# An attention and Fourier-mixing kernel: a shallower pair pipeline, row means from the residual add, held loads, and Fourier pieces emitted together

## The chip, the cores and the metric

One core of a Trainium2 chip runs the whole problem. The time is device microseconds (us) of one execution; the kernel before has a median of 345.32 us over 3 runs (344.11 to 345.38). Engines are named as the profile names them: PE is TensorE (PEld its weight loads), DVE VectorE, ACT ScalarE, POOL GpSimd, SP SyncE, which here only issues DMAs.

## What is computed

Block-sparse attention for 4 batches of 8 heads (768 positions, head size 64), then a Fourier mixing layer and a two-layer network over the 512 features that the heads form together. Inputs and output are float32.

```python
k_rep = k.reshape(B, H, 12, 64, D).mean(axis=3)
gate_scores = q . k_rep, with later blocks set to -1e9
sel = the 3 best blocks of each row, and its own block
attn = softmax(q k^T / 8, over the selected blocks and causal)   # then attn @ v
x = attn output as (batch, 768, 512)
u = x + real(fft over features of (fft over positions of x))
un = (u - mean(u)) / sqrt(var(u) + 1e-6)        # over the 512 features
out = u + relu(un @ w_ch1) @ w_ch2
```

## The kernel before

Heads are taken two at a time: 16 pairs P, four to a batch b. A pair goes through these stages, each a Python function that emits instructions.

- `stage_A(P)` transposes k and then q by PE (12 transposes, L239). For k, DVE sums the blocks (L242, `kr`) and ACT copies the tile to float16 (L245 for pairs under 7, L248 after); for q, DVE copies (L253) and POOL converts (L170).
- `stage_G(P)` is the gate: PE scores each row against the blocks (L300 or L266), and DVE turns them into a mask: a transpose, ten or twelve MAX8, two small products and a transpose (L307 to L315, or L272 to L281).
- `stage_S(P, 0)` to `stage_S(P, 5)` are the six score tiles: PE (L339, L344, masks L350), exponential on ACT (L354), causal edge on POOL (L357).
- `stage_V(P, 0)` and `(P, 1)` multiply with v on PE (L370); after the second, DVE takes the reciprocal (L379) and writes x (L167 `x`). `stage_fold` prepares the Fourier input on DVE (`sd` for each pair, `zw` for the third and fourth pair of a batch).

When all four pairs of a batch are folded its stream follows: `stage_fg` (DVE), `stage_Y(b, 0)` and `(b, 1)` (PE L423 and L429, out by ACT L436 `ty` and DVE L438 `tr`), `stage_M(b, 0)` to `(b, 2)`, `stage_R` (the reciprocal square root, DVE and POOL), 16 `stage_W1` tiles (L503, L505; ReLU on ACT L512 or DVE L510) and 6 `stage_W2` tiles (L521; DVE adds the residual at L527, SP stores at L530). `stage_M(b, kp)` covers 256 rows: 8 matmuls, one DVE add `u = mixed + x` of 1024 columns (L458), two `bn_stats` and `bn_aggr` (L468, L469), the scaled mean (L471), two ACT passes that write the centred rows (L474), and two DMA transposes on SP into `unT` (L477). W1 needs `unT`. In L167 `u` is that add, because all such adds share one helper line.

All PSUM tiles come from one pool of four buffers (`pst`), each two banks: a fifth tile waits for one of the four before it to be read.

What sets the order. `attn_slot(i, g, a)` lists the pieces of one slot: scores of pair i, gate of pair g, `stage_A` of pair a with its loads for pair a + 3 behind it, and `stage_V` of pair i - 1. Before, g is i + 2 and a is i + 3 up to slot 3, slot 4 has no `stage_A`, slot 5 has no gate, and from slot 6 on they are i + 1 and i + 2. Slots 0 to 4 run alone. From slot 5 on `weave` mixes the slots of four pairs with one batch's stream, by the weights that stand beside each piece; `stream` also puts the last four W2 tiles of the batch before (`held`) behind `stage_fg` and `stage_R`. The opening (L669 to L682) runs in exactly the order written on all engines; after it only SP does, and on the other engines Tile's scheduler takes the pieces by their place in the list and by what its plan says is ready. SP issues every load of q, k and v (`load`, L216 and L209) and every `unT` transpose, so a load emitted ahead of a transpose is issued ahead of it. W1 and W2 weights are loaded by POOL in four chunks each, gated on a pair's scores (`load_w1`, `load_w2`).

Of the kernel before, what the change touches and what calls it, by code (L numbers as in the profile page):

```python
# [20 lines left out]
DM = 512  # L21
# [107 lines left out]
def kernel(  # L129
# [99 lines left out]
    def stage_A(P):  # L229
# [5 lines left out]
        for who in (1, 0):  # L235
# [4 lines left out]
            if who == 1:  # L240
# [3 lines left out]
                if P < NX:  # L244
                    nc.scalar.copy(out=qk[:, 1, XW(P), :], in_=ps)  # L245
                else:
                    for e in range(2):
                        nc.scalar.copy(out=qk[0:64, e, 1, :], in_=ps[64 * e:64 * e + 64])  # L248
# [194 lines left out]
    def stage_M(b, kp):  # L443
# [3 lines left out]
        for k2 in range(2):  # L447
# [9 lines left out]
        kk = slice(2 * kp, 2 * kp + 2)  # L457
        tt(u_b.rearrange("p k (m two) -> p k two m", two=2),  # L458
           mps.rearrange("p k (two m) -> p k two m", two=2),
           x_b[:, kk, :].rearrange("p k (m two) -> p k two m", two=2), ALU.add)  # L460
        if kp == 0:
            un_t[b] = bpool.tile([128, NDT, S], F16, tag="unT", name=f"unT_{b}", bufs=1)
            st_t[b] = [bpool.tile([128, *sh], FP, tag=n, name=f"{n}_{b}", bufs=2)
                       for n, sh in (("mv", [NST, 2]), ("rs", [NST]))]
        mv = st_t[b][0]
        for k2 in range(2):
            bst = spool.tile([128, 6], FP, tag="bst", name=f"bst{2 * kp + k2}_{b}", bufs=4)
            nc.vector.bn_stats(out=bst, in_=u_b[:, k2, :])  # L468
            nc.vector.bn_aggr(out=mv[:, 2 * kp + k2, :], in_=bst)  # L469
        nm = spool.tile([128, 2], FP, tag="nm", name=f"nm{kp}_{b}")  # L470
        nc.vector.tensor_scalar(out=nm, in0=mv[:, kk, 0], scalar1=-0.0625, scalar2=None,  # L471
                                op0=ALU.mult)
# [103 lines left out]

    def load_w1(dt, P):
# [12 lines left out]
    def attn_slot(i, g, a):  # L590
# [78 lines left out]
    with tc.manual_schedule(engines={ET.SP, ET.PE, ET.DVE, ET.Activation, ET.Pool}):  # L669
# [62 lines left out]
```

## Time and profile before

| What | Value |
|---|---|
| median of 3 runs | 345.32 us (344.11 to 345.38) |
| the profiled execution's own time | 343.65 us |
| its span, first to last instruction | 341.9 us |
| busy: PE, DVE, ACT, POOL | 304.9, 190.4, 164.7, 114.7 us |
| mean granted TensorE clock | 0.955 of full |

A profile row gives a time from the start of the span, a duration, and in square brackets how long the engine was idle before it and what ended that. PE's ends are modelled, so PE can be shown busy for somewhat longer than a matmul holds it. In the rows by stretch each engine has its busy time and, in brackets, its instructions; PEclk is the granted clock as a share of 2.4 GHz, so 0.50 is 1.2 GHz throughout.

### The profile page before, as it was taken

How to read it: one execution, taken by the hardware profiler on the slowest of the kernel's cores; microseconds unless marked ns; L12 is line 12 of the kernel's file. 1: busy time of each engine (PE TensorE's matmuls, PEld its weight loads, DVE VectorE, ACT ScalarE, POOL GpSimd, SP SyncE). 2: the span in 40 equal slices, each digit the busy share in tenths (PEclk: the TensorE clock that was granted, in tenths of full speed). 3: DMA queues.
4: the chain of work that ended last, by engine and by line, in shares of the span. 5: the costliest groups of instructions: out<-in, count | busy, mean ns of one | idle time of the engine just before them, and what ended most of it. 6: DMA issues, size and time to landing. Idle time of an engine off the chain costs nothing.

```text
span 341.9 us, 6605 instructions
## 1 busy us (share of the span) xinstructions
PE 304.9 (89%) x2594; PEld 180.1 (53%) x2594; DVE 190.4 (56%) x534; ACT 164.7 (48%) x203; POOL 114.7 (34%) x257
## 2 busy tenths in 40 slices
PE   7579787776999999969999999989999999599994
PEld 3356554454556555725666555645665463266441
DVE  2678886597457367892546376974414478021211
ACT  2327776448486643473757634375664024145000
POOL 2436467535544443336362423245110001100000
PEclk9859998896999999989999999999999999899999
DMA  9999999993772544039930004045000102600022
GB/s 175 219 229 265 229 213 211 217 179 65 138 140 46 105 92 110 3 61 229 188 63 0 2 0 110 2 94 169 0 2 0 63 0 58 159 0 2 0 82 104
DMA packets 95371, 34.40 MB, mean 101 GB/s; under 512 B 89120, under 2 KB 91500, under 8 KB 95340
## 3 DMA queue, kind: packets, MB, share of 16 engines
q1 hardware_dynamic: 90460, 29.26, 40.2%
q0 software_dynamic: 2688, 4.19, 6.9%
q10 hardware_dynamic: 2192, 0.52, 0.8%
q8 instruction: 20, 0.33, 0.4%
q14 instruction: 11, 0.09, 0.1%
HBM read 28.73 MB, written 6.29 MB: 102 GB/s over the span
## 4 chain that ended last, share of the span: by engine, by line
PE 67%; DVE 21%; ACT 7%; issue 2%; DMA 2%; SPq 0%; POOL 0%; DVEq 0%
PE c L521 18%; PE h L503 16%; PE h L505 8%; PE av L370 5%; PE sc L344 5%; DVE bst L468 4%; DVE u L167 3%; PE tp L239 2%; PE yp L423 2%; DVE kr L242 2%; DVE x L167 2%; DMA unT<-x 2%; PE g L300 2%; PE sc L339 2%; ACT pt L354 2%
## 5 line engine op out<-in xcount | busy, mean ns | idle before, releaser
L354 ACT ACTIVATE pt<-sc 128x1024 f16<-128x1024 f32 x96 | 84.8, 920 | 46.7 <-PE sc L344 37.8
L521 PE MATMUL c<-w_sb,hT 128*128 128x512 f16 x384 | 88.2, 382 | 1.7 <-ACT pt L354 1.1
L503 PE MATMUL h<-unT,w_sb 128*128 128x512 f16 x256 | 87.1, 385 | 1.8 <-DMA unT<-x 1.8
L505 PE MATMUL h<-unT,w_sb 128*128 128x256 f16 x256 | 69.9, 276 | 2.5 <-DMA unT<-x 2.5
L357 POOL TENSOR_SCALAR_AFFINE_SELECT pt<-pt 128x256 f16<-128x256 f16 x96 | 40.2, 426 | 92.6 <-ACT pt L354 91.8
L521 PEld LDWEIGHTS <-hT 128*128 128x128 f16 x384 | 37.3, 98 | 44.5 <-issue 4.2
L512 ACT ACTIVATE hT<-h 128x768 f16<-128x768 f32 x48 | 38.7, 812 | 36.2 <-PE h L505 35.8
L510 DVE TENSOR_SCALAR hT<-h 128x768 f16<-128x768 f32 x16 | 15.3, 956 | 48.2 <-PE h L505 48.2
L503 PEld LDWEIGHTS <-w_sb 128*128 128x128 f16 x256 | 25.2, 99 | 30.4 <-issue 4.6
L527 DVE SCALAR_TENSOR_TENSOR u<-c,rs,u 128x512 f32<-128x512 f32 x24 | 17.1, 742 | 35.5 <-PE c L521 35.5
L170 POOL TENSOR_SCALAR_AFFINE_SELECT qk<-q 64x768 f16<-64x768 f32 (+1 forms) x25 | 21.6, 866 | 28.0 <-DVE q L253 24.7
L344 PE MATMUL sc<-qk 96*128 96x512 f16 (+3 forms) x144 | 27.8, 306 | 2.7 <-DVE q L253 1.3
L505 PEld LDWEIGHTS <-w_sb 128*128 128x128 f16 x256 | 25.3, 99 | 8.4 <-DMA unT<-x 3.5
L370 PEld LDWEIGHTS <-pt 128*128 128x128 f16 x672 | 25.9, 100 | 5.7 <-issue 1.5
L239 PE MATMUL tp<-id,nat 128*128 128x128 f32 x192 | 26.4, 285 | 2.6 <-issue 1.6
L370 PE MATMUL av<-v,pt 128*128 128x65 f16 x672 | 28.0, 198 | 0.3 <-POOL pt L357 0.3
L474 ACT ACTIVATE x<-u,nm 128x512 f16<-128x512 f32 x24 | 15.8, 713 | 20.7 <-DVE nm L471 20.7
L239 PEld LDWEIGHTS tp<-id,nat 128*128 128x128 f32 x192 | 22.0, 146 | 6.5 <-issue 3.7
L339 PE MATMUL sc<-qk 64*128 64x512 f16 (+3 forms) x112 | 16.7, 338 | 7.6 <-ACT qk L245 3.9
L170 POOL TENSOR_SCALAR_AFFINE_SELECT qk<-mt 32x384 f16<-32x384 f16 x36 | 18.3, 508 | 7.5 <-DVE mt L281 5.8
L344 PEld LDWEIGHTS <-qk 96*128 96x128 f16 x144 | 12.9, 97 | 12.1 <-issue 3.3
L248 ACT CAST qk<-tp 64x768 f16<-64x768 f32 x18 | 14.3, 792 | 8.7 <-DVE kr L242 8.6
(81 smaller groups left out, 335.6 us busy)
## 6 DMA issues: line engine op xcount, KB each, us to landing
nat<-in_k_dram SPq DMA_DIRECT2D x32, 192.0 KB, 4.4
nat<-in_v_dram SPq DMA_DIRECT2D x16, 384.0 KB, 6.4
nat<-in_q_dram SPq DMA_DIRECT2D x30, 192.0 KB, 4.3
out_dram<-u SPq DMA_DIRECT2D x11, 512.0 KB, 3.3
w_sb<-in_moe_w_ch_dram POOLq DMA_DIRECT2D x8, 512.0 KB, 7.4
fs_sb<-c_FS SPq DMA_DIRECT2D x1, 582.0 KB, 4.8
out_dram<-u SPq DMA_DIRECT2D x2, 256.0 KB
nat<-in_q_dram ACTq DMA_DIRECT2D x2, 192.0 KB, 5.4
```

What stands on the lines that cost most here:

```text
L170: nc.gpsimd.affine_select(out=out, in_=in_, pattern=[[0, i] for i in n], base=0, channel_multiplier=0, compare_op=ALU.is_ge, fill=0.0)
L239: nc.tensor.transpose(ps[:, 128 * st:128 * st + 128], src[:, st, :], id32)
L339: nc.tensor.matmul(ps[:, e, co:co + q1 - q0], qk[hs[e], 1, XW(P), 128 * jt:128 * jt + 128], qk[hs[e], 0, XW(P), q0:q1], start=(co == 0), s ...
L344: nc.tensor.matmul(ps[:, e, co:co + q1 - q0], qk[0:96, e, 1, 128 * jt:128 * jt + 128], qk[0:96, e, 0, q0:q1], start=True, stop=True)
L354: nc.scalar.activation(out=pt[:, o:o + 2 * n].rearrange("p (e c) -> p e c", e=2), in_=ps[:, :, 0:n], func=AF.Exp, scale=0.125)
L357: nc.gpsimd.affine_select(out=dg, in_=dg, pattern=[[0, 2], [1, 128]], base=0, channel_multiplier=-1, compare_op=ALU.is_ge, fill=0.0)
L370: nc.tensor.matmul(av[:, e, 66 * st:66 * st + 65], pt[:, co:co + 128], vv[:, e, jt, 0:65], start=(cnt == 0), stop=(cnt == 20))
L503: nc.tensor.matmul(hp[:, 0:512], w1s, unT[:, dt, 0:512], start=(dt == 0), stop=(dt == NDT - 1))
L505: nc.tensor.matmul(hp[:, 512:768], w1s, unT[:, dt, 512:768], start=(dt == 0), stop=(dt == NDT - 1))
L512: nc.scalar.activation(out=hT, in_=hp, func=AF.Relu)
L521: nc.tensor.matmul(cps[:, part, :], h_t[b, it][:, 128 * st:128 * (st + 1)], w2_sb[:, it, :], start=(it == 0), stop=(it == NIT - 1))
L527: nc.vector.scalar_tensor_tensor(out=o[:, i, :], in0=cps[:, i, :], scalar=st_t[b][1][:, sts[i]:sts[i] + 1], in1=o[:, i, :], op0=ALU.mult, ...
```

## The change

Four things are altered.

1. The order of the pairs. The opening emits all six score tiles of pair 0 between `stage_G(1)` and the end of `stage_A(2)`, and the ACT copy of k of pair 1 is emitted after the first two of them (`later`). Slot 0 is gone. Slots 1 to 4, and all after, take gate i + 1 and `stage_A` i + 2. Inside a slot `stage_A` moves up to behind `stage_S(i, 1)`, and each half of `stage_V` moves back by one score tile.
2. `stage_M` has, for each half of 512 columns, one scalar_tensor_tensor whose accumulator gives the row sum, where one 1024-wide add, two bn_stats and two bn_aggr stood; the scaled mean comes from that sum. The bn_stats and bn_aggr move to `stage_R`.
3. `hold_loads` and `free_loads`: SP's loads that fall between them go on a list and are issued behind the batch's last `unT` transpose. In batch 0 holding starts at slot 4.
4. Weights in `stream`: `stage_Y` 0.5 for 1.3, `stage_M` 0.3 for 0.87, `stage_R` 10 (batch 0) or 3 for 6 or 1, so that the Y and M pieces come closer together in the list and W1 comes later. W2's chunks are gated on pairs 5 and 6, not 4 and 5.

```diff
     def load(P, who, eng):
+        if hold[0] is not None:
+            hold[0].append((P, who, eng))
+            return
...
                 if P < NX:
-                    nc.scalar.copy(out=qk[:, 1, XW(P), :], in_=ps)
+                    cp = (lambda ps=ps: nc.scalar.copy(out=qk[:, 1, XW(P), :], in_=ps))
+                    if later is None:
+                        cp()
+                    else:
+                        later.append(cp)
...
-        tt(u_b.rearrange("p k (m two) -> p k two m", two=2),
-           mps.rearrange("p k (two m) -> p k two m", two=2),
-           x_b[:, kk, :].rearrange("p k (m two) -> p k two m", two=2), ALU.add)
...
         for k2 in range(2):
-            bst = spool.tile([128, 6], FP, tag="bst", name=f"bst{2 * kp + k2}_{b}", bufs=4)
-            nc.vector.bn_stats(out=bst, in_=u_b[:, k2, :])
-            nc.vector.bn_aggr(out=mv[:, 2 * kp + k2, :], in_=bst)
+            kt = 2 * kp + k2
+            nc.vector.scalar_tensor_tensor(
+                out=u_b[:, k2, :].rearrange("p (m two) -> p two m", two=2),
+                in0=mps[:, k2, :].rearrange("p (two m) -> p two m", two=2), scalar=1.0,
+                in1=x_b[:, kt, :].rearrange("p (m two) -> p two m", two=2),
+                op0=ALU.mult, op1=ALU.add, accum_out=sm[:, kt:kt + 1])
         nm = spool.tile([128, 2], FP, tag="nm", name=f"nm{kp}_{b}")
-        nc.vector.tensor_scalar(out=nm, in0=mv[:, kk, 0], scalar1=-0.0625, scalar2=None,
-                                op0=ALU.mult)
+        nc.vector.tensor_scalar(out=nm, in0=sm[:, 2 * kp:2 * kp + 2],
+                                scalar1=-0.0625 / DM, scalar2=None, op0=ALU.mult)
...
     def stage_R(b):
-        mv, rs = st_t[b]
+        mv, rs, _ = st_t[b]
+        for kt in range(NST):
+            bst = spool.tile([128, 6], FP, tag="bst", name=f"bst{kt}_{b}", bufs=4)
+            nc.vector.bn_stats(out=bst, in_=u_t[b, kt // 2][:, kt % 2, :])
+            nc.vector.bn_aggr(out=mv[:, kt, :], in_=bst)
...
+    def hold_loads():
+        hold[0] = hold[0] or []
+
+    def free_loads():
+        L, hold[0] = hold[0], None
+        for x in L or []:
+            load(*x)
...
         add(i - 1, 0.0, lambda: cast_v(i - 1))
-        if i > 0:
-            add(i, 0.45, lambda: stage_S(i, 0))
+        add(i, 0.45, lambda: stage_S(i, 0))
         add(g, 0.4, lambda: stage_G(g))
-        if i > 0:
-            add(i, 0.45, lambda: stage_S(i, 1))
+        add(i, 0.45, lambda: stage_S(i, 1))
+        add(a, 1.3, sa)
+        add(i, 0.45, lambda: stage_S(i, 2))
         add(i - 1, 0.6, lambda: stage_V(i - 1, 0))
         if g is not None and g >= NX:
             add(g, 0.0, lambda: stage_K(g))
-        add(i, 0.45, lambda: stage_S(i, 2))
+        add(i, 0.45, lambda: stage_S(i, 3))
         add(i - 1, 0.6, v1)
-        add(i, 0.45, lambda: stage_S(i, 3))
-        add(a, 1.3, sa)
         add(i, 0.45, lambda: stage_S(i, 4))
         add(i, 0.12, lambda: stage_S(i, 5))
...
-        L = [(lambda: stage_fg(b), 0.0)] + held[0:1]
-        L += [(lambda h=h: stage_Y(b, h), 1.3) for h in range(2)]
-        L += [(lambda kp=kp: stage_M(b, kp), 0.87) for kp in range(3)]
-        L += [(lambda: stage_R(b), 6.0 if b == 0 else 1.0)]
+        L = [(hold_loads, 0.0), (lambda: stage_fg(b), 0.0)] + held[0:1]
+        L += [(lambda h=h: stage_Y(b, h), 0.5) for h in range(2)]
+        L += [(lambda kp=kp: stage_M(b, kp), 0.3) for kp in range(3)]
+        L += [(free_loads, 0.0), (lambda: stage_R(b), 10.0 if b == 0 else 3.0)]
         L += held[1:]
         if b == 0:
-            L += [(lambda c=c: load_w2(c, 4 + c // 2), 0.0) for c in range(4)]
+            L += [(lambda c=c: load_w2(c, 5 + c // 2), 0.0) for c in range(4)]
...
-        stage_A(1)
+        later = []
+        stage_A(1, later)
         stage_S(0, 0)
         stage_S(0, 1)
+        later[0]()
         stage_G(1)
         kq(4)
         load(1, 2, nc.sync)
+        stage_S(0, 2)
+        stage_S(0, 3)
         stage_A(2)
+        stage_S(0, 4)
+        stage_S(0, 5)
...
-        run(attn_slot(0, 2, 3))
         load_w1(0, 0)
-        run(attn_slot(1, 3, 4))
+        run(attn_slot(1, 2, 3))
...
-        run(attn_slot(4, 6, None))
+        hold_loads()
+        run(attn_slot(4, 5, 6))
...
-                L += attn_slot(i, *((None, 7) if i == 5 else (i + 1, i + 2)))
+                L += attn_slot(i, i + 1, i + 2)
```

## Rows read from the trace of the kernel before

**Rows 1.** The page: the span and each engine's busy time.

```profile
span 341.9 us, 6605 instructions
PE 304.9 (89%) x2594; PEld 180.1 (53%) x2594; DVE 190.4 (56%) x534; ACT 164.7 (48%) x203; POOL 114.7 (34%) x257
```

**Rows 2.** By stretch: start:end, length, PE, PEld, DVE, ACT, POOL, clock, DMA, GB/s.

```profile
28.00:35.60 7.60, 6.50 (x110) 4.38 (x104) 6.00 (x21) 5.93 (x8) 4.96 (x11) 1.00 1.14 281
43.20:51.90 8.70, 6.64 (x108) 4.47 (x104) 7.34 (x23) 6.93 (x10) 5.81 (x13) 1.00 1.08 215
73.00:79.00 6.00, 2.10 (x23) 1.43 (x23) 6.00 (x13) 4.58 (x7) 2.51 (x4) 1.00 0.53 104
79.00:86.20 7.20, 5.83 (x68) 3.45 (x65) 4.72 (x24) 4.79 (x7) 5.11 (x17) 0.54 0.39 61
146.00:150.00 4.00, 2.06 (x11) 0.78 (x8) 4.00 (x11) 3.30 (x6) 1.29 (x2) 1.00 0.17 33
150.00:154.00 4.00, 2.90 (x19) 0.92 (x18) 3.55 (x17) 3.45 (x5) 1.53 (x4) 0.66 0.49 100
170.00:205.00 35.00, 34.97 (x300) 21.46 (x299) 19.13 (x56) 20.56 (x26) 14.43 (x26) 1.00 0.13 22
220.00:225.00 5.00, 3.93 (x26) 2.42 (x25) 5.00 (x15) 3.51 (x6) 0.41 (x1) 1.00 0.26 52
292.00:298.00 6.00, 3.52 (x14) 1.54 (x12) 0.00 (x0) 0.43 (x1) 0.22 (x2) 0.72 0.76 203
```

**Rows 3.** Timeline, PE and DVE, opening and slot 1: start, us, instruction, [idle before].

```profile
17.00 2.82 PE L239 MATMUL tp<-id,nat 128*128 128x128 f32 x12
29.05 0.52 DVE L307 STREAM_TRANSPOSE gt<-g 128x320 f32<-128x320 f32 x1 [1.32 <-PE g L304]
30.72 0.81 PE L370 MATMUL av<-v,pt 128*128 128x65 f16 x21
32.83 0.63 DVE L167 TENSOR_TENSOR sd<-x 128x384 f16<-128x384 f16 x2
35.21 0.39 PE L339 MATMUL sc<-qk 64*128 64x512 f16 x2 [1.10 <-ACT qk L245]
36.59 0.52 DVE L307 STREAM_TRANSPOSE gt<-g 128x320 f32<-128x320 f32 x1 [1.31 <-PE g L304]
```

**Rows 4.** The chain that ended last, 56 to 90 us: start, us, what.

```profile
60.65 0.64 DVE fg L167
66.84 1.04 ACT ty L436
78.49 0.85 DVE kr L242
82.89 3.25 DMA unT<-x
```

**Rows 5.** Groups by line: count | busy us, mean ns of one | idle before.

```profile
L468 DVE BATCH_NORM_STATS2 bst<-u 128x6 f32<-128x512 f32 x24 | 15.4, 677 | 0.0
L469 DVE BATCH_NORM_AGGREGATE mv<-bst 128x2 f32<-128x6 f32 x24 | 3.7, 166 | 0.0
L167 DVE TENSOR_TENSOR u<-mx,x 128x1024 f32<-128x1024 f32 x12 | 14.3, 1205 | 0.0
L527 DVE SCALAR_TENSOR_TENSOR u<-c,rs,u 128x512 f32<-128x512 f32 x24 | 17.1, 742 | 35.5 <-PE c L521 35.5
```

**Rows 6.** One line, the transposes into unT: count, duration ns min/median/max.

```profile
L477 SPq DMA_TRANSPOSE unT<-x x24: 1189/1217/2141, 73.6 to 291.6; - x24
```

**Rows 7.** The chain from 275 to 300 us, then PE's timeline there.

```profile
279.35 2.32 DVE u L167 x2
291.58 3.53 DMA unT<-x
...
295.15 0.40 PE L505 MATMUL h<-unT,w_sb 128*128 128x256 f16 x1 [2.48 <-DMA unT<-x]
```

**Rows 8.** Timeline of POOL at 49 us: v's cast and its load.

```profile
49.09 0.90 POOL L170 TENSOR_SCALAR_AFFINE_SELECT v<-nat 128x768 f16<-128x768 f32 x1 [0.17 <-DMA nat<-in_v_dram]
```

More of the change, by code (lines that the diff above doesn't have):

```diff
@@ L202 @@
     x_t, u_t, un_t, h_t, st_t = {}, {}, {}, {}, {}
+    hold = [None]
     def load(P, who, eng):
+        if hold[0] is not None:
+            hold[0].append((P, who, eng))
+            return
         b, hp = divmod(P, NP)
@@ L227, in XW, with stage_A @@
         return 1 if P in (0, 1, 2, 6) else 0
-    def stage_A(P):
+    def stage_A(P, later=None):
         d = pairs[P]
@@ L456, in stage_M @@
                                  stop=True)
-        kk = slice(2 * kp, 2 * kp + 2)
-        tt(u_b.rearrange("p k (m two) -> p k two m", two=2),
-           mps.rearrange("p k (two m) -> p k two m", two=2),
-           x_b[:, kk, :].rearrange("p k (m two) -> p k two m", two=2), ALU.add)
         if kp == 0:
@@ L463, in stage_M @@
             st_t[b] = [bpool.tile([128, *sh], FP, tag=n, name=f"{n}_{b}", bufs=2)
-                       for n, sh in (("mv", [NST, 2]), ("rs", [NST]))]
-        mv = st_t[b][0]
+                       for n, sh in (("mv", [NST, 2]), ("rs", [NST]), ("sm", [NST]))]
+        sm = st_t[b][2]
         for k2 in range(2):
-            bst = spool.tile([128, 6], FP, tag="bst", name=f"bst{2 * kp + k2}_{b}", bufs=4)
-            nc.vector.bn_stats(out=bst, in_=u_b[:, k2, :])
-            nc.vector.bn_aggr(out=mv[:, 2 * kp + k2, :], in_=bst)
+            kt = 2 * kp + k2
[4 more added lines that the diff above has]
+                op0=ALU.mult, op1=ALU.add, accum_out=sm[:, kt:kt + 1])
         nm = spool.tile([128, 2], FP, tag="nm", name=f"nm{kp}_{b}")
-        nc.vector.tensor_scalar(out=nm, in0=mv[:, kk, 0], scalar1=-0.0625, scalar2=None,
-                                op0=ALU.mult)
+        nc.vector.tensor_scalar(out=nm, in0=sm[:, 2 * kp:2 * kp + 2],
+                                scalar1=-0.0625 / DM, scalar2=None, op0=ALU.mult)
         for k2 in range(2):
@@ L686 @@
         nc.sync.dma_start(fd_sb, dr["FD"].ap())
-        run(attn_slot(0, 2, 3))
         load_w1(0, 0)
-        run(attn_slot(1, 3, 4))
+        run(attn_slot(1, 2, 3))
         load_w1(1, 1)
-        run(attn_slot(2, 4, 5))
+        run(attn_slot(2, 3, 4))
         load_w1(2, 2)
-        run(attn_slot(3, 5, 6))
+        run(attn_slot(3, 4, 5))
         load_w1(3, 3)
         consts_next()
-        run(attn_slot(4, 6, None))
+        hold_loads()
+        run(attn_slot(4, 5, 6))
         for b in range(B):
```

## The prediction, made before the change was run

> **What bounds the kernel now.** I read the page first: PE is busy 304.9 us of a span of 341.9 [rows 1], so the first question is where the other 37 us lie, and where PE runs at half clock. Busy time by stretch answers that. From 170 to 205 us PE is full at the granted clock of 1.00 [rows 2]; of such stretches (86 to 130 and 298 to 325 look the same) nothing can be won by moving work. The idle time sits in five other places, each with a limit of its own.
>
> First the attention-only stretch, up to the first Fourier piece at 60.65 us [rows 4]. A slot there takes 7.54 us, from one gate transpose at 29.05 to the next at 36.59 [rows 3], with PE busy 6.50, DVE 6.00, ACT 5.93 of 7.6 [rows 2]: no engine is full. DVE waits 1.3 us for the gate's matmuls once a slot and PE waits 1.10 us for the ACT copy of k to free a PSUM buffer [rows 3]. It is a loop of dependences: gate, mask, x, fold, k sums, copy of k, next scores. Slot 3, where the fold has a second step, takes 8.7 us [rows 2].
>
> Then the Fourier chain of each batch, read in the chain that ended last and in the same stretches. For batch 0 it runs from 60.65 to the last transpose landing at 82.89 + 3.25 = 86.1 us, 25.5 us, and other work stands in it: the k sums of the next pair at 78.49, ahead of the last rows' mean [rows 4]. DVE is full from 73 to 79 while PE is idle 3.9 us, and the next 7.2 us have 1.4 idle at a clock of 0.54 [rows 2]. Batch 1 shows the same from 146 to 154 (3.0 idle, the second half at 0.66), batch 2 has 1.1 from 220 to 225 [rows 2]. In batch 3 nothing is left beside the chain but W2: W1's second matmul group waits 2.48 us for `unT` at 295.15 [rows 7], and the stretch after 292 runs at 0.72 [rows 2].
>
> **The change, part by part.**
>
> (a) Shallower pairs. The opening now holds the scores of pair 0, so one whole slot goes; its gate 2 and pair 3 move to slot 1, where old slot 1 had gate 3 and pair 4, and gate 6 moves behind the Y pieces. In the opening pair 2's 12 transposes ran from 17.00 to 19.8 [rows 3]. They now stand behind two score tiles, estimated at 0.8 each (twice the 0.39 us of such a tile [rows 3], the most that the lower clock level can make of it), and behind a gate that may be up to 1.0 later, as the copy of k follows two exponentials. So they end near 22.4, and with the copy of q slot 1 starts near 23.6. A new slot lies between PE's 6.50 [rows 2] and, if a new loop closes, 8.1 (rival 1). `stage_A` in front of V lets the next gate's matmuls run while DVE does x and the fold, so the old 1.3 us wait should shrink to about 0.9, while PE no longer queues behind the k copy at the slot's start: I take 7.2, and 8.1 for the two slots with the second fold step. Then the Fourier pieces start at 23.6 + 7.2 + 7.2 + 8.1 + 8.1 = 54.2, 6.4 ahead of 60.65; less gate 6 on PE, which comes later (some 0.8 of the 1.4 us from 35.21 to 36.59 [rows 3]), **5.6**. With 6.5 a slot (plus 0.9 twice) it is 10, with 8.1 (plus 0.9 twice) it is 2.8; less 0.8 each, 2 to 9.
>
> (b) Means from the add. Before, a half of u cost DVE one add (1205 ns for 1024) and for each 512 a bn_stats of 677 and a bn_aggr of 166 in front of the mean [rows 5]; back to back, some 1.1 + 2 x (0.6 + 0.08) = 2.5 us for each of three. After it is two scalar_tensor_tensor. The nearest row is the W2 residual: also PSUM and SBUF in, float32 out, 742 ns, without accumulator [rows 5]. The accumulator is not in the trace: I bound it by nothing and by a second pass (0.74), and take 0.16, what bn_aggr takes for a few columns. So 2 x (0.66 + 0.1) = 1.5 us: the chain loses 1.0 for each of three, 3 us a batch (with a second pass it gains 0.3 each). The six bn_stats and bn_aggr, 4.1 us, move to `stage_R`, whose result only W2's residual uses, over 10 us later; they cost nothing on that path, but DVE serves them ahead of the next pair's k sums, which is a price where DVE is full. The Trainium skill (Vector Engine (DVE) Microarchitecture Reference, Points that are easy to get wrong) says that a scalar_tensor_tensor with two SBUF sources wider than bf16 runs at half throughput, as no read port is left for the accumulator; here one source is PSUM and the other float16, and the residual's 742 ns for 512 columns [rows 5] is full rate. By that rule, were it to bite, the add would be slower than the part it replaces (rival 4).
>
> (c) Pieces together, loads held. Without pair 7's k sums between them [rows 4] the three halves follow one another, and then SP is next: six transposes at 1.2 us each [rows 6] from the first x on, 7.5 us with gaps, plus a landing of 3.3 to 3.5 [rows 4, 7]. From fg: 6.2 to the second `ty` as before (66.84 - 60.65 [rows 4]) and 1 for it, 2 to 3 for gate 6 and the first u, 1 for x, 7.5, and 2.3 more for the last landing: 20 to 21 where it was 25.5. Held loads (v5, k and q of 9, v6) cost nothing while SP has no need of them: they follow at about 73, and v5 is first used in slot 6, near 80. Without the hold they would stand ahead of the transposes in SP's queue.
>
> What that is worth where PE has other work: batch 0 had 5.3 idle and 7.2 us at 0.54, but DVE has as much to do as before, so **2.5** (0 to 5); batch 1 **2.5** of 3.0 idle and the slow clock (0 to 4); batch 2 **1** (0 to 1.5). Batch 3: from 279.35 [rows 7], 1.6 for the first two adds and 0.9 for mean and x, so transposes from 281.9 to 289.5 and the last one landed near 291.5 instead of 295.1; W2 covers PE up to its wait as before, and the time at 0.72 shrinks too: **3.5** (2 to 5).
>
> **The sum.** 5.6 + 2.5 + 2.5 + 1 + 3.5 = 15.1. The profiled execution took 343.65 (span 341.9, 1.75 around it): 343.65 - 15.1 = 328.5. The median of the runs is 1.67 above that execution, so **330** is the forecast. Low ends give 4, high ends 24.5.
>
> **Rivals.**
>
> 1. A new loop in the slot. With four PSUM buffers in turn the fourth score tile waits for the copy of k, the second half of V stands behind that tile, and the next slot's first tile takes V's buffer, free only after x. This loop is the old one without the fold (0.63) and with half of V (0.81) and a score tile (0.39) [rows 3]: 7.54 - 0.63 + 0.81 + 0.39 = 8.1 us. For it: the 1.10 us wait [rows 3] shows PSUM buffers biting. Against it: the scheduler may place V ahead of the tile that can't start. The slots then bring 2.0 instead of 5.6: 333.5.
> 2. The gain in batches 0 to 2 is hidden: DVE, full from 73 to 79 and 146 to 150 [rows 2], has the same work, and bn_stats now stand before the next pair's pieces, so PE waits there instead. Then only (a) and batch 3 count, 9.1: 336.
> 3. Loads. POOL's cast of v3 at 49.09 already waited for its DMA [rows 8], with the DMA engines full there (share 1.08 and more, 215 to 281 GB/s [rows 2]). If v3 and pair 6 cannot land earlier than before, the cast, and so slot 4's V, stays at 50 and fg comes near 57: (a) brings 3: 332.5. Against it: v now stands ahead of k and q in SP's order.
> 4. Slower. The accumulating add takes twice its time (1.4 us). Then a half costs 2.8 plus, later, 1.36 for its bn_stats: DVE has 3 x 1.7 = 5 us more in each batch, in the very stretches where it is full, and attention waits behind it. Batches 0 to 2 lose 5 each instead of winning 6 in all, batch 3 keeps 0: 343.65 - 5.6 + 15 + 1.67 = 354.7. It decides from about 1.1 us an add on; against it the residual's 742 ns.
> 5. The scheduler undoes the closeness (its plan, not the list, decides among ready pieces; it already mixed in pair 7's sums): (a) and half of batch 3, 7.4: 338.
>
> **How the numbers follow.** Forecast 0.48 (its own range 323 to 334), rival 1 0.18, rival 2 0.12, rival 3 0.08, rival 5 0.06, rival 4 0.08. The range, 323 to 340, leaves out rival 4 and the forecast's outer ends. A measurement of this kernel tells about 0.5%, 1.7 us, from no change. Faster than 343.6: all but rival 4 and a few hundredths of the others, 0.87; within 0.5%: 0.05; slower: 0.08.
>
> **What would show it.** Right: the first fg near 54 us, slots of about 7.2 between gate transposes, adds at about 0.75 us with a short read of the accumulator behind each, six transposes back to back on SP at 1.2 to 1.3 us, and in batch 3 PE's last wait for `unT` under 1.5 us. Rival 1: PE idle once a slot before a score tile, ended by ACT's copy of k or DVE's x, slots of 8. Rival 2: DVE full and PE idle behind `stage_R`. Rival 3: POOL or PE idle, ended by a DMA of `nat`, before 55 us. Rival 4: adds of 1.1 us or more. The forecast is wrong if the first fg is later than 58, or if PE's idle time after 60 us is not smaller than before.

## The result, and the profile after

The changed kernel takes 331.09 us in the median of four runs (330.59 to 333.89), the kernel before 345.35 us beside it (344.11 to 346.15): a ratio of 0.961, with a 95% interval of 0.955 to 0.967. The profiled execution of the changed kernel took 331.54 us, 12.1 less than that of the kernel before (343.65).

First the same two rows of the page as in [rows 1].

```profile
span 329.8 us, 6632 instructions
PE 299.6 (91%) x2594; PEld 178.9 (54%) x2594; DVE 191.4 (58%) x570; ACT 165.3 (50%) x203; POOL 114.9 (35%) x257
```

The span is 12.1 us shorter. PE's idle time fell from 37.0 to 30.2 us, and its busy time by 5.3 us, for the same 2594 matmuls. The second part is the clock: its mean over the span is 0.974, and was 0.955. DVE's busy time did not fall. Its 36 more instructions are 12 more adds and 24 reads of the accumulator.

Then busy time by stretch, cut where the first `fg` piece of each batch starts (start:end, length, PE, PEld, DVE, ACT, POOL, clock, DMA, GB/s). Of the kernel before:

```profile
0.00:60.65 60.65, 46.23 (x548) 28.50 (x548) 41.27 (x143) 33.40 (x40) 31.48 (x74) 0.89 1.15 220
60.65:127.70 67.05, 60.17 (x565) 37.84 (x566) 41.87 (x114) 39.65 (x49) 31.43 (x64) 0.92 0.63 121
127.70:204.00 76.30, 72.06 (x608) 43.31 (x606) 46.56 (x137) 41.91 (x52) 30.90 (x65) 0.98 0.36 75
204.00:273.50 69.50, 67.06 (x553) 39.45 (x552) 37.53 (x98) 33.96 (x42) 18.52 (x45) 1.00 0.21 54
273.50:341.90 68.40, 59.33 (x325) 31.01 (x323) 23.12 (x44) 15.78 (x20) 2.38 (x12) 0.98 0.17 51
```

Of the changed kernel:

```profile
0.00:57.58 57.58, 43.77 (x536) 27.81 (x536) 39.31 (x130) 33.21 (x40) 29.38 (x70) 0.93 1.10 215
57.58:127.40 69.82, 64.07 (x594) 39.73 (x595) 45.80 (x140) 42.34 (x52) 35.33 (x71) 0.93 0.75 142
127.40:200.40 73.00, 70.62 (x608) 42.92 (x607) 46.67 (x145) 42.48 (x52) 30.82 (x64) 1.00 0.33 76
200.40:264.90 64.50, 63.35 (x537) 37.85 (x535) 36.33 (x105) 31.61 (x39) 16.98 (x41) 1.00 0.19 49
264.90:329.80 64.90, 57.76 (x325) 30.57 (x323) 23.26 (x53) 15.70 (x20) 2.40 (x12) 1.00 0.19 53
```

These tables split the gain. The opening is 60.65 - 57.58 = 3.1 us shorter. From the first `fg` to that of batch 3 it is 212.85 against 207.32, 5.5 shorter. Batch 3 and the tail are 68.4 - 64.9 = 3.5 shorter. Together 12.1.

Within the 5.5 the batches differ. Batch 1 has the same 608 matmuls and is 3.3 us shorter: 1.9 less idle time on PE and 1.4 less busy time, at a clock of 1.00 for 0.98. The stretch of batch 0 is 2.8 longer and that of batch 2 is 5.0 shorter, but the first holds 29 matmuls more and the second 16 fewer, as work moved between them; PE's idle time fell by 1.1 us in batch 0 (6.9 to 5.8) and by 1.3 in batch 2 (2.4 to 1.2).

In the opening DVE's timeline has one gate transpose a slot (start, us, instruction, idle time before it in brackets).

```profile
23.20 0.52 DVE L316 STREAM_TRANSPOSE gt<-g 128x320 f32<-128x320 f32 x1 [1.10 <-PE g L313]
30.55 0.50 DVE L316 STREAM_TRANSPOSE gt<-g 128x320 f32<-128x320 f32 x1
37.64 0.52 DVE L316 STREAM_TRANSPOSE gt<-g 128x320 f32<-128x320 f32 x1 [0.41 <-PE g L313]
49.02 0.50 DVE L316 STREAM_TRANSPOSE gt<-g 128x320 f32<-128x320 f32 x1
```

The chain that ended last runs through the third of these slots (start, us, what):

```profile
32.79 8.36 DMA nat<-in_v_dram
```

And so does PE's timeline:

```profile
42.16 0.80 PE L379 MATMUL av<-v,pt 128*128 128x65 f16 x21 [2.07 <-POOL v L170]
```

The first slots take 7.35 and 7.09 us, where [rows 3] has 7.54. The third takes 11.4: V of pair 2 waits for its `v`, whose load SP requested at 32.79 us only and which took 8.4 us to land; POOL's cast follows it.

The chain of batch 0 on DVE (timeline, same columns):

```profile
66.33 0.65 DVE L473 SCALAR_TENSOR_TENSOR u<-mx,x 128x512 f32<-128x512 f32 x1
66.91 0.08 DVE L473 DVE_READ_ACCUMULATOR u<-mx,x 128x1 f32 x1
66.91 0.81 DVE L319 MAX8 mx<-gt 128x8 f32<-128x12 f32 x10
...
71.15 0.68 DVE L473 SCALAR_TENSOR_TENSOR u<-mx,x 128x512 f32<-128x512 f32 x1
71.76 0.69 DVE L492 BATCH_NORM_STATS2 bst<-u 128x6 f32<-128x512 f32 x1
```

And on SP:

```profile
69.59 7.93 SPq L485 DMA_TRANSPOSE unT<-x  x6
77.62 0.53 SPq L214 DMA_DIRECT2D nat<-in_v_dram  x1
```

Six adds lie between 66.33 and 71.8, with gate 6's small steps between them (MAX8 among others) and no bn_stats; those follow at 71.76. The six transposes go out back to back, 69.59 to 77.5, where before they stretched from 73.6 to 85.0. The held load of `v` comes right behind them.

And batch 3, PE's timeline. Of the kernel before, the wait ahead of the one in [rows 7]:

```profile
291.66 1.02 PE L503 MATMUL h<-unT,w_sb 128*128 128x512 f16 x4 [1.79 <-DMA unT<-x]
```

Of the changed kernel:

```profile
281.11 0.38 PE L515 MATMUL h<-unT,w_sb 128*128 128x512 f16 x1
283.85 0.28 PE L517 MATMUL h<-unT,w_sb 128*128 128x256 f16 x1 [2.37 <-DMA unT<-x]
```

Before, PE waited twice for `unT`, 1.79 and 2.48 us; now it waits once, 2.37. The end of the wait comes 19.0 us after this batch's `fg` where it took 21.7, and the clock stays at 1.00 behind it (in the stretch of [rows 2] that begins at 292 it was 0.72).

### The profile page after: what moved, and what is told of

The parts are those of the page before. It is cut to its first block, busy times and chain, and to the rows that moved or that the text cites. A ratio compares the mean times of both kernels' runs of the same rounds, so it can differ in the third digit from the quotient of the medians.

```text
span 329.8 us, 6632 instructions
## 1 busy us (share of the span) xinstructions
PE 299.6 (91%) x2594; PEld 178.9 (54%) x2594; DVE 191.4 (58%) x570; ACT 165.3 (50%) x203; POOL 114.9 (35%) x257
## 4 chain that ended last, share of the span: by engine, by line
PE 67%; DVE 17%; ACT 7%; DMA 4%; issue 2%; SPq 1%; POOL 1%; DVEq 0%
PE c L533 19%; PE h L515 17%; PE h L517 9%; PE sc L353 5%; PE av L379 4%; PE tp L244 3%; DMA nat<-in_v_dram 3%; ACT x L482 2%; PE yp L432 2%; ACT pt L363 2%; DVE u L473 2%; PE warmps L558 2%; DVE zw L167 2%; DVE kr L247 2%; PE sc L348 2%
## 5 line engine op out<-in xcount | busy, mean ns | idle before, releaser
L363 ACT ACTIVATE pt<-sc 128x1024 f16<-128x1024 f32 x96 | 84.7, 916 | 56.5 <-PE sc L353 42.0
L533 PE MATMUL c<-w_sb,hT 128*128 128x512 f16 x384 | 86.9, 379 | 0.3 <-ACT pt L363 0.3
L515 PE MATMUL h<-unT,w_sb 128*128 128x512 f16 x256 | 85.8, 380 | 0.6 <-ACT pt L363 0.6
L366 POOL TENSOR_SCALAR_AFFINE_SELECT pt<-pt 128x256 f16<-128x256 f16 x96 | 41.5, 443 | 79.0 <-ACT pt L363 78.6
L379 PE MATMUL av<-v,pt 128*128 128x65 f16 x672 | 26.6, 195 | 3.6 <-POOL v L170 2.1
L379 PEld LDWEIGHTS <-pt 128*128 128x128 f16 x672 | 24.4, 98 | 9.6 <-issue 5.5
L170 POOL TENSOR_SCALAR_AFFINE_SELECT qk<-q 64x768 f16<-64x768 f32 (+1 forms) x25 | 20.6, 825 | 16.3 <-DVE q L262 15.1
L244 PE MATMUL tp<-id,nat 128*128 128x128 f32 x192 | 24.5, 276 | 0.7 <-DVE tr L447 0.3
L170 POOL TENSOR_SCALAR_AFFINE_SELECT v<-nat 128x768 f16<-128x768 f32 x16 | 15.1, 944 | 26.0 <-DMA nat<-in_v_dram 25.9
L244 PEld LDWEIGHTS tp<-id,nat 128*128 128x128 f32 x192 | 21.2, 141 | 3.8 <-issue 1.5
L348 PE MATMUL sc<-qk 64*128 64x512 f16 (+3 forms) x112 | 16.4, 335 | 6.3 <-ACT qk L250 2.9
L257 ACT CAST qk<-tp 64x768 f16<-64x768 f32 x18 | 14.3, 794 | 9.6 <-DVE kr L247 9.5
```

Of the source, the lines that this page charges most:

```text
L170: nc.gpsimd.affine_select(out=out, in_=in_, pattern=[[0, i] for i in n], base=0, channel_multiplier=0, compare_op=ALU.is_ge, fill=0.0)
L244: nc.tensor.transpose(ps[:, 128 * st:128 * st + 128], src[:, st, :], id32)
L348: nc.tensor.matmul(ps[:, e, co:co + q1 - q0], qk[hs[e], 1, XW(P), 128 * jt:128 * jt + 128], qk[hs[e], 0, XW(P), q0:q1], start=(co == 0), s ...
L363: nc.scalar.activation(out=pt[:, o:o + 2 * n].rearrange("p (e c) -> p e c", e=2), in_=ps[:, :, 0:n], func=AF.Exp, scale=0.125)
L366: nc.gpsimd.affine_select(out=dg, in_=dg, pattern=[[0, 2], [1, 128]], base=0, channel_multiplier=-1, compare_op=ALU.is_ge, fill=0.0)
L379: nc.tensor.matmul(av[:, e, 66 * st:66 * st + 65], pt[:, co:co + 128], vv[:, e, jt, 0:65], start=(cnt == 0), stop=(cnt == 20))
```

## The experiments

Three theories were to be told apart. The first is the prediction's: the parts add up, each with its own worth. The second is rival 3: the opening is held by DMA traffic, and that alone took 3 us from the forecast. The third: the parts need each other, so that one alone brings little or harms. Twelve kernels were run, in four groups; each but one has a ratio to the kernel before from runs on the same chip.

**Means alone.** The kernel before, with the adds and `stage_R` of the changed kernel:

```diff
-            nc.vector.bn_stats(out=bst, in_=u_b[:, k2, :])
-            nc.vector.bn_aggr(out=mv[:, 2 * kp + k2, :], in_=bst)
...
+            nc.vector.scalar_tensor_tensor(
...
+                op0=ALU.mult, op1=ALU.add, accum_out=sm[:, kt:kt + 1])
```

> The kernel before with one edit: the mean comes from the accumulator of the residual add, and bn_stats moves to the end of the chain. The working in the prediction takes 1.0 us off each half of u. That is 2 to 3 us in batch 3, where only W2 is left beside the chain, and 0 to 1 us in each other batch, so 340 to 343 us. Rival: the means are worth little while the next pair's pieces stand between the halves; the waits only move, and the time stays at 344 to 346. In the trace each add should take 0.65 to 0.75 us, followed by a short read of the accumulator.

Measured: 338.98 us (337.42 to 339.61), ratio 0.976 (0.969 to 0.983): the gain is larger than the 340 to 343 expected. The groups by line (count | busy us, mean ns of one | idle before):

```profile
L464 DVE SCALAR_TENSOR_TENSOR u<-mx,x 128x512 f32<-128x512 f32 x24 | 15.6, 683 | 0.0
L464 DVE DVE_READ_ACCUMULATOR u<-mx,x 128x1 f32 x24 | 2.0, 82 | 0.0
```

An add with its accumulator takes 0.68 us and the read 0.08; the second pass that rival 4 feared does not exist.

**Depth alone.** The kernel before, with the changed opening, `attn_slot` and main loop, and W2's chunks gated on pairs 5 and 6:

```diff
-        run(attn_slot(0, 2, 3))
-        run(attn_slot(1, 3, 4))
+        run(attn_slot(1, 2, 3))
...
-                L += attn_slot(i, *((None, 7) if i == 5 else (i + 1, i + 2)))
+                L += attn_slot(i, i + 1, i + 2)
```

> The kernel before with the shallower pairs and the new opening, but bn_stats in the chain, no held loads and the old spacing of the Fourier pieces. By the prediction's sum the first fg comes 6.4 us earlier, at 54, and the time falls by 5.6 to about 340. By what the trace of the changed kernel shows (V of pair 2 waits for its load, first fg at 57.6) the first fg comes 3 us earlier and the time falls by 2 to 4, to 341 to 343. Third theory: without held loads the shallow order makes the next pair's k and q loads collide with the transposes, and nothing is won: 344 to 346.

Measured: 354.29 us (349.31 to 356.49), ratio 1.017 (1.008 to 1.026): slower, which none of the three had. The profiled execution took 349.31, the least of the four. The first `fg` does come earlier, at 56.5. PE's waits for `unT` from there to 91 us (us in total, times, longest):

```profile
PE h L507 <- DMA unT<-x: 11.5, 1, 11.5
PE h L509 <- DMA unT<-x: 2.0, 1, 2.0
```

W1's first group stands in PE's queue ahead of the next pair's attention, and `unT` comes late: 13.5 us idle at one place, more than the depth can win. **Depth and hold** adds only the held loads:

```diff
+        if hold[0] is not None:
+            hold[0].append((P, who, eng))
+            return
...
-        L = [(lambda: stage_fg(b), 0.0)] + held[0:1]
+        L = [(hold_loads, 0.0), (lambda: stage_fg(b), 0.0)] + held[0:1]
...
-        L += [(lambda: stage_R(b), 6.0 if b == 0 else 1.0)]
+        L += [(free_loads, 0.0), (lambda: stage_R(b), 6.0 if b == 0 else 1.0)]
```

> The shallower depth with held loads, and nothing else of the change: plain add and bn_stats in the chain, the old spacing of the pieces. The depth alone took 354.3 us against 346.8 for the kernel before, with PE waiting 11.5 us for unT in batch 0: the loads of v6 and pairs 8 and 9 were requested up to 74.3 us, the first transpose at 74.40, the last two took 7 us to land. If these loads made the depth alone slow, the last transpose lands before 86 here instead of 89, PE waits 4 to 7 us, and the time is 345 to 349. Rival: DVE is what is late (the halves of u end at 75 with bn_stats between), the wait stays over 9 us, and the time is 351 to 355.

Measured: 349.26 us (348.13 to 353.09), ratio 1.011 (1.007 to 1.015). The median is 5 us below the depth alone, but the two intervals overlap and the two profiled executions are only 1.2 us apart (348.13 and 349.31); the wait only falls to 11.3. Neither expectation holds whole. POOL's timeline (start, us, what):

```profile
76.43 0.78 POOL L600 DMA_DIRECT2D w_sb<-in_moe_w_ch_dram  x1
77.39 0.78 POOL L600 DMA_DIRECT2D w_sb<-in_moe_w_ch_dram  x1
```

SP's:

```profile
72.14 8.16 SPq L486 DMA_TRANSPOSE unT<-x  x6
80.40 0.56 SPq L214 DMA_DIRECT2D nat<-in_v_dram  x1
```

And what PE waits for, up to 91 us:

```profile
PE h L512 <- DMA unT<-x: 7.6, 1, 7.6
PE h L514 <- DMA unT<-x: 3.7, 1, 3.7
```

SP has issued the last transpose at 80.3, but PE can go on at 88.5 only, 8 us later. In the changed kernel the issue ended at 77.5 and W1's second part ran without a wait at 80.7, 3 us later. Both have the held loads right behind; one thing that differs is that two chunks of W2's weights are requested at 76.4 and 77.4 here, with the transposes still out, and at 83.8 and 85.4 in the changed kernel, where `stage_R`'s weight of 10 puts them later. The depth alone shows the same: chunks at 77.8 and 78.8, the last transpose issued by 82.9, PE going on at 89.0. The Trainium skill (DMA: Bandwidth & Descriptors, Queues, rings and completion order) says that a DMA engine takes turns, packet by packet, between the queues that have work; the 8 us beside POOL's chunks agree with that. That the chunks alone do it was not tried.

**One part undone at a time.** Four kernels take one part out of the changed kernel. Means undone (bn_stats back in `stage_M`, as in the first diff, reversed):

> The changed kernel with the plain add, bn_stats and bn_aggr back in the chain for the mean; depth, held loads and close pieces as in the changed kernel. If DVE sets the pace of the chain (2.5 us a half against 1.5), each chain is some 3 us longer and the gain that the means brought alone (339.0 against 346.8, 7.8 us) is lost again: 336 to 340 us. Rival: with the pieces close together SP sets the pace, two transposes of 1.25 us for each half; then only the first half's 1 us shows in each batch: 332 to 334.

Measured: 339.08 us (338.89 to 340.82), ratio 0.981 (0.975 to 0.986): 8.0 above the changed kernel, so DVE sets the pace. In batch 3 `fg` to the last landing takes 22.1 us instead of 19.0, the 3 us that the prediction took, and the clock adds to it. The stretch of batch 3 (columns as above):

```profile
285.00:290.00 5.00, 1.87 (x8) 0.77 (x9) 0.00 (x0) 0.00 (x0) 0.60 (x4) 0.81 0.80 163
290.00:295.00 5.00, 5.00 (x18) 2.52 (x17) 0.00 (x0) 1.62 (x2) 0.00 (x0) 0.51 0.27 103
295.00:300.00 5.00, 5.00 (x33) 3.03 (x31) 0.96 (x1) 2.43 (x3) 0.00 (x0) 1.00 0.00 0
```

PE is idle 4.7 us there (1.7 and 3.0, for `unT`), and then does 18 matmuls in 5 us at 0.51 where the next 5 us hold 33 at 1.00. So the wait is paid again in clock here. No load held:

```diff
     def hold_loads():
-        hold[0] = hold[0] or []
+        hold[0] = None
```

> The changed kernel, with no load held back. In the kernel with the depth alone the next loads (k, q and v, ten requests between 58 and 74 us) stood ahead of the transposes in SP's queue, the last two transposes took 7.3 us to land, and PE waited 11.5 us for unT. If the hold is what prevents this, the same is seen here: transposes of batch 0 start at 73 to 75 instead of 69.6, the last lands after 85, and the time is 335 to 341. Rival: it was DVE's work between the halves (bn_stats, pieces apart) that made the chain late there; then the transposes still start at 70 to 71 here and the time is 331 to 333.

Measured: 337.94 us (336.17 to 339.91), ratio 0.978 (0.971 to 0.985), 6.8 above the changed kernel. SP's timeline:

```profile
65.16 4.36 SPq L214 DMA_DIRECT2D nat<-in_v_dram  x1
69.64 9.59 SPq L485 DMA_TRANSPOSE unT<-x  x6
```

And ACT's, for the first two rows of centred `x`:

```profile
66.58 1.34 ACT L482 ACTIVATE x<-u,nm 128x512 f16<-128x512 f32 x2 [0.54 <-DVE nm L479]
```

SP stands in the request of a `v` from 65.16 to 69.52 (the one at 77.62 above takes 0.53), so the first transpose goes out 3.06 us after ACT begins the rows (69.64 - 66.58). In the changed kernel that is 0.75 (69.59, where ACT begins at 68.84). From `fg` (56.1) to PE's going on with the last landing (81.8) it is then 25.7 us, against at most 23.1. The expected times, a start at 73 to 75 and a landing after 85, did not come, in part because this kernel's `fg` is 1.5 earlier, but the mechanism is the one expected: 2.3 us late behind a load. Over batch 0 (56.1 to 130.1) PE is idle 3.2 us more than in the changed kernel (8.9 against 5.8), 2.9 of it one wait for `unT`, and busy 1.0 more for the same 594 matmuls: the clock is 0.63 to 0.79 in the 12 us behind 76, where the changed kernel has 4 us at 0.65 and 4 at 0.92. The profiled execution is 4.6 above that of the changed kernel (336.17 against 331.54).

Old spacing of the Fourier pieces:

```diff
-        L += [(lambda h=h: stage_Y(b, h), 0.5) for h in range(2)]
-        L += [(lambda kp=kp: stage_M(b, kp), 0.3) for kp in range(3)]
-        L += [(free_loads, 0.0), (lambda: stage_R(b), 10.0 if b == 0 else 3.0)]
+        L += [(lambda h=h: stage_Y(b, h), 1.3) for h in range(2)]
+        L += [(lambda kp=kp: stage_M(b, kp), 0.87) for kp in range(3)]
+        L += [(free_loads, 0.0), (lambda: stage_R(b), 6.0 if b == 0 else 1.0)]
```

> The changed kernel with the old spacing of the Fourier pieces (1.3, 0.87 and 6.0 or 1.0 in place of 0.5, 0.3 and 10.0 or 3.0). If the closeness is what takes the next pair's pieces out of the chain, the chain from fg to the last transpose's landing grows by 2 to 4 us in each of batches 0 to 2 and the time is 333 to 337. Rival: the scheduler orders by what is ready, and DVE's order hardly differs: 330 to 332.5.

Measured: 337.41 us (333.24 to 337.63), ratio 0.972 (0.964 to 0.980), 6.3 above the changed kernel in the median, though the intervals overlap (0.964 to 0.980, and 0.955 to 0.967). DVE's timeline has the next pair's k sums and q copy ahead of the first add:

```profile
66.99 0.95 DVE L247 TENSOR_REDUCE kr<-tp 128x12 f32<-128x768 f32 x1
68.08 0.95 DVE L262 COPY q<-tp 128x768 f32<-128x768 f32 x1
69.37 0.65 DVE L473 SCALAR_TENSOR_TENSOR u<-mx,x 128x512 f32<-128x512 f32 x1
```

From `fg` (58.33) to the first add it is 11.0 us, in the changed kernel 8.75 (66.33 - 57.58): 2.3 us more. To the last landing (PE goes on at 83.07) it is 24.7, against at most 23.1: at least 1.6 us, where 2 to 4 was expected. Depth undone, the old opening and slots (and W2's chunks gated on pairs 4 and 5 again) with all the rest kept:

> The changed kernel at the old depth: the old opening and slot order, with means, held loads and close pieces kept. The shallower depth moved the first fg by 3.1 us, so if its worth is this shift alone, the time is 334 to 335.5. If it also takes work out of the chain of batch 0 (gate 6 and the k sums), 336 to 339. Rival: the depth is worth nothing by itself, as the kernel with the depth alone is slower than the kernel before; then 330 to 332.

Measured: 345.37 us (343.71 to 376.03), ratio 0.997 (0.993 to 1.001): the whole gain is gone, more than any theory had. PE's timeline:

```profile
84.51 1.32 PE L379 MATMUL av<-v,pt 128*128 128x65 f16 x21 [4.28 <-POOL v L170]
```

POOL's:

```profile
83.55 0.90 POOL L170 TENSOR_SCALAR_AFFINE_SELECT v<-nat 128x768 f16<-128x768 f32 x1 [4.02 <-DMA nat<-in_v_dram]
```

At the old depth PE reaches V of that pair before the held `v` is there. So **old depth, no load held**, which is the kernel above with the empty `hold_loads` of the diff before:

> The old depth with means and close pieces, but no load held back. With the held loads this kernel took 345.4 us, 6.4 more than the kernel before with the means alone (339.0); its trace shows PE waiting 4.3 us for the cast of a v whose load was held back to 78 us. If the hold is what costs this at the old depth, 337 to 340 here. Rival: the close pieces cost it, as the gate of pair 7 is pushed behind the chain and PE runs out of attention work; then 343 to 346.

Measured: 342.66 us (341.17 to 343.72), ratio 0.990 (0.985 to 0.994), between the two. The hold costs 2.7 us at the old depth, though the intervals touch. With no load held this kernel does nothing that the means alone (338.98) does not, except for the weights of the pieces, so the close pieces cost the other 3.7 there. Which pieces then stand in whose way was not followed further. Against the kernel with no load held (337.94), which differs from this one in the depth alone, the new depth is worth 4.7 us.

**The opening's traffic.** The changed kernel with w1 requested later:

```diff
-        load_w1(0, 0)
         run(attn_slot(1, 2, 3))
-        load_w1(1, 1)
         run(attn_slot(2, 3, 4))
-        load_w1(2, 2)
+        load_w1(0, 2)
         run(attn_slot(3, 4, 5))
-        load_w1(3, 3)
+        load_w1(1, 3)
...
         run(attn_slot(4, 5, 6))
+        load_w1(2, 4)
+        load_w1(3, 4)
```

> The changed kernel with the four chunks of w1 (0.5 MB written, 1 MB read each) requested two slots later or more: chunk 0 behind pair 2's scores, chunk 1 behind pair 3's, chunks 2 and 3 behind pair 4's. If the opening is bound by DMA traffic, v of pair 2 lands 3 to 5 us before its 41.15, the wait of V of pair 2 (2.07 us) goes, the first fg comes at 54 to 56 and the time falls by 1.5 to 3.5, to 327.5 to 329.5. Rival 1: PE then waits for the copy of k or for x once a slot, slots take 8.1, the first fg stays at 57 and the time at 331. Rival 2: the late chunks hold up W1 of batch 0 near 80 us or the transposes beside it, and what is won is given back: 331 to 333.

Measured: 330.31 us (326.91 to 331.84), ratio 0.951 (0.945 to 0.956). DVE's timeline, gates and first `fg`:

```profile
23.28 0.52 DVE L316 STREAM_TRANSPOSE gt<-g 128x320 f32<-128x320 f32 x1 [1.10 <-PE g L313]
37.72 0.52 DVE L316 STREAM_TRANSPOSE gt<-g 128x320 f32<-128x320 f32 x1 [0.41 <-PE g L313]
46.24 0.50 DVE L316 STREAM_TRANSPOSE gt<-g 128x320 f32<-128x320 f32 x1
54.86 0.56 DVE L167 TENSOR_TENSOR fg<-zw 128x762 f16<-128x762 f16 x1
```

And PE's, near the end:

```profile
281.25 0.28 PE L517 MATMUL h<-unT,w_sb 128*128 128x256 f16 x1 [2.75 <-DMA unT<-x]
283.43 0.63 PE L515 MATMUL h<-unT,w_sb 128*128 128x512 f16 x1
286.30 0.38 PE L515 MATMUL h<-unT,w_sb 128*128 128x512 f16 x1
```

The wait for `v` is gone, the third slot takes 8.5 instead of 11.4, and the first `fg` comes at 54.9, as the theory of DMA traffic has it. Yet the median is only 0.8 us below that of the changed kernel, and the intervals of the ratios overlap (0.945 to 0.956, and 0.955 to 0.967). In the profiled executions batch 3 and the tail take 67.0 us here instead of 64.9. PE's wait for `unT` at the end is followed by 3.3 us at a granted clock of 0.50, matmuls of 0.63 us between ones of 0.38, which the profiled execution of the changed kernel does not have. Most of what the opening won (2.7 us) is given back there. With the Fourier tables moved as well:

```diff
-        nc.sync.dma_start(fs_sb, dr["FS"].ap())
-        nc.sync.dma_start(fd_sb, dr["FD"].ap())
         run(attn_slot(1, 2, 3))
+        nc.sync.dma_start(fs_sb, dr["FS"].ap())
+        nc.sync.dma_start(fd_sb, dr["FD"].ap())
```

> As the kernel with w1 later, and the two Fourier tables (0.97 MB, first used after fg) are also requested behind slot 1's loads instead of ahead of them. In the queue v of pair 2 then follows q of pair 5 at about 28 us instead of 32.8. If the place in the queue is what counts, v lands at 34 to 37, the first fg is at 54 to 55 and the time 327 to 329. If only the total traffic counts, the tables push v of pair 3 back by as much, V of pair 3 waits instead, and the time is that of the kernel with w1 later alone.

Measured: a median of 331.57 us in six runs; their spread, 326.06 to 356.0, leaves no interval, and the time decides nothing. The trace does: first `fg` at 55.1, the third slot 8.6. Behind w1 the place of the tables no longer matters to them.

**Filling the last wait.** The kernel with w1 later, and in batch 3 the first three W1 groups take columns 0 to 511, which need four of the six transposes, ahead of columns 512 to 767:

```diff
-    def stage_W1(b, it):
+    def stage_W1(b, its):
         unT = un_t[b]
-        hp = pst([128, S], f"h{it}_{b}")
-        for dt in range(NDT):
...
+        hps = [pst([128, S], f"h{it}_{b}") for it in its]
+        for lo, hi in ((0, 512), (512, 768)):
+            for hp, it in zip(hps, its):
+                for dt in range(NDT):
...
+                    nc.tensor.matmul(hp[:, lo:hi], w1s, unT[:, dt, lo:hi], start=(dt == 0),
+                                     stop=(dt == NDT - 1))
```

> The kernel with w1 later, and in batch 3 the first three groups of W1 take their columns 0 to 511 first and 512 to 767 behind them. In the kernel with w1 later PE waited 2.75 us for the last transposes at 278.5 and its clock fell to 1.2 GHz 1.1 us after it took up again, for 3.4 us, which cost 1.5 to 2 us. If that wait is what lowers the clock, 12 matmuls of 0.22 us (2.6 us) now stand in it, the wait is under 0.5 us, the clock stays at 2.4 GHz, and the time falls by 2.5 to 4.5 us, to 325.5 to 328. Rival: the clock falls whatever PE does there (the transposes' traffic, or the waits before), then only the 2.6 us of work moved are gained less what the slow stretch takes: 328 to 329.5. Second rival: columns 0 to 511 wait for the last transposes too, as these land together, and nothing changes: 330.

Measured: 326.43 us (325.04 to 326.64), ratio 0.942 (0.939 to 0.946): faster than the changed kernel; against the kernel with w1 later the intervals just touch. PE's timeline:

```profile
277.98 2.75 PE L517 MATMUL h<-unT,w_sb 128*128 128x512 f16 x12
280.98 1.48 PE L517 MATMUL h<-unT,w_sb 128*128 128x256 f16 x12 [0.24 <-DMA unT<-x]
```

And the stretch (columns as above):

```profile
280.00:285.00 5.00, 4.76 (x33) 2.98 (x32) 0.96 (x1) 2.21 (x3) 0.54 (x3) 1.00 0.59 210
```

The wait is 0.24 us where it was 2.75, and the clock stays at 1.00. Batch 3 and the tail take 62.9 us, 4.1 less than in the profiled execution with w1 later alone: 2.5 less idle time, and 1.7 less busy time for the same 325 matmuls, which is the clock. The same in all four batches:

> As the kernel with the halves in batch 3, for all four batches. In batch 0 PE waits 1 to 1.4 us for the last transposes near 78 us with its clock at 1.2 GHz; batches 1 and 2 show no such wait. So batch 0 gains 1 to 2 us: 324.5 to 327. Rival: three PSUM buffers held at once keep the next pair's score tiles out, and batches 0 to 2 lose 0.5 to 1 us each: 327 to 330.

Measured: 326.66 us (323.57 to 328.7), ratio 0.942 (0.937 to 0.946), no different. In batch 0 this kernel's trace, like that of the one before it, shows no wait for `unT` on PE; there was nothing to fill.

## Why the prediction was right, and where it was not

The time was forecast as 330 and is 331.09. By its own steps:

**(a) Shallower pairs, 5.6 (6.4 up to the first `fg`): mis-sized, 3.1.** Slots of 7.2 were forecast, 7.35 and 7.09 came, and slot 1 started earlier than the 23.6 taken. What failed is "7.2 + 7.2 + 8.1 + 8.1": the third slot took 11.4 (the fourth 8.6). That is rival 3, with its sign (PE idle behind POOL's cast and a DMA of `nat`), its place (`v`, pair 2's and not pair 3's) and its size (`fg` near 57; it was 57.58). The argument against it, that `v` now stands ahead of k and q in SP's queue, overlooked that k and q of pair 5 and the two Fourier tables stand ahead of `v` of pair 2, and that w1 shares the engines. With w1 later the third slot takes 8.5 and `fg` is at 54.9, 0.7 from the 54.2 forecast: so most of what is missing is the load. But the slots did not get shorter. From the gate transpose at 23.28 to `fg` at 54.86 the four take 31.6 us, as the old four did (60.65 - 29.05), where 30.6 was forecast; what (a) brings is the start, 5.8 us earlier. The 8.7 read for the old slot 3 is the width of a stretch: from gate to gate it was 9.15 (44.14 to 53.29), and the one behind it 7.36. Two slips change nothing: with 6.5 a slot the sum gives 9.2 and not 10, so the high ends give 23.9 and not 24.5; and, other than the list of changes says, two of pair 0's six tiles stand ahead of `stage_G(1)` as before, two behind it and two behind `stage_A(2)`. Rival 1's wait (PE for the copy of k) is there too, but smaller: 2.9 us in four places up to 57.58, against 3.9 before.

**(b) Means from the add: right in size.** 0.68 and 0.08 us an add where 0.66 and 0.1 were taken; the accumulator's read is the 82 ns row, below the 0.16 taken. The Trainium skill's rule on two non-bf16 SBUF sources (Vector Engine (DVE) Microarchitecture Reference, Points that are easy to get wrong) does not bite with one source in PSUM: 682 ns with the accumulator against 740 for W2's residual add without one. Float16 is not bf16 either, so it is the PSUM source alone that keeps this add out of the rule. The 3 us a batch show in batch 3 (19.0 us, and 22.1 with the means undone).

**(c) Pieces together, loads held: right in place.** Six transposes back to back at 1.2 to 1.3 in batch 0; at most 23.1 us from `fg` to the last landing in batch 0, where 20 to 21 was forecast and 25.5 before. From the first `fg` to that of batch 3 the forecast was 6.0, less the 0.8 for gate 6 that comes later, so 5.2; it is 5.5. Batch 1 brings 3.3 where 2.5 was forecast; batches 0 and 2, between which work moved, bring 2.2 together where 3.5 less 0.8 was. Batch 3: 3.5 forecast, 3.5 measured. But the sign "PE's last wait for `unT` under 1.5 us" did not come: it is 2.37. W2 does cover PE as before, for 16.2 us behind `fg` (281.11 - 264.9) where it was 16.4 (291.66 - 1.79 - 273.5), but the last landing comes 19.0 us behind `fg` where 18.0 was forecast (291.5 - 273.5). The prediction also read only the second of the old waits. Of the 3.5 only 1.9 is less idle time (9.1 against 7.1: 4.3 us of waits before, 2.4 now), and 1.6 is less busy time (59.33 against 57.76): the clock, which stayed at 1.00 in this execution. That part is luck, as the kernel with w1 later shows. Neither sign of being wrong came: the first `fg` is 0.4 short of 58, and PE's idle time behind it is 16.4 us where it was 22.6.

**The sum.** 15.1 was forecast against the profiled execution, 12.1 came, and the missing 3 are (a)'s. That the median is still met within 1.1 us is luck in one respect: 1.67 was added because the first profile lay below its median, while the second lies 0.45 above.

**What no step said.** The prediction summed the parts as if each had its own worth. Taken out one at a time, against the 331.09 of the changed kernel, they are worth 8.0 (means), 6.8 (hold), 6.3 (close pieces) and 14.3 (depth), 35 in all where the change brings 14. The kernel before took 345.4 to 346.8 on the chips used; by the ratios to it the four come to some 29, so this is no difference of chips. Alone, the means bring 7.8, and the depth loses 7.5. The depth takes the next pair's pieces away from PE's queue ahead of W1, so a late `unT` leaves PE with nothing; it pays where means and close pieces bring `unT` early, 4.7 us with no load held and 14.3 with the hold. The hold pays 6.8 at the new depth and costs 2.7 at the old, where the `v` that it delays is needed first; the close pieces too cost 3.7 at the old depth. The prediction's step "held loads cost nothing while SP has no need of them" held for this depth alone.

## What to carry to other kernels

Ask of each part of a schedule change what it takes cover away from: a shallower pipeline pays only if the chain it uncovers is shortened in the same step. Where the compute engines look free, count the bytes in flight, for a load requested in time can still land 8 us later. And a wait of 2 to 3 us on TensorE can cost more than itself, for the clock may fall behind it (1.7 us on top of 2.5 with w1 later, though not each time), so fill it with work that needs only the part of the data that is there.

## What the runs showed of the hardware

- A DMA request can hold its issuing queue: SP's request of a `v` takes 0.53 us in the median of 16 in the changed kernel, up to 2.5 there, and 4.36 with no load held, in 4 us at a DMA share of 1.18; a transpose behind it waits. Busy DMA engines alone do not do it: the request at 32.79 took 0.38, at a share of 1.13 (30 to 36 us).
- The length of PE's wait does not tell whether the clock falls behind it. At one place, the wait for `unT` in batch 3, the granted clock fell to between 0.50 and 0.63 in stretches of 2 to 3.3 us behind waits of 2.75 (w1 later), 2.60 (old depth, no load held), 2.55 (no load held) and 2.41 (tables moved too). It stayed at 1.00 behind waits of 2.75 (old spacing), 2.59 (depth undone) and 2.37 (the changed kernel). What decides is open.
- With q, k, v and w1 in flight the opening moves 215 GB/s over 57.58 us at a DMA share of 1.10; with w1 later it is 214 GB/s over 54.86 at 1.11. Asking for w1 later shortened it by 2.7 us; moving the tables too did not. Single stretches moved up to 281 GB/s [rows 2], so 215 is not shown to be a limit.
